# Sharing the first weight load of a DMA-filled decode kernel between two queues

## The chip, the core and the metric

One core of one Trainium2 chip. The metric is the device time of one execution of the kernel in microseconds (us), as a median over runs. All times within the trace are counted from the start of the span, which is about 2 us shorter than the device time of the same run.

## The reference

The reference is one decode step with its gradients: a pre-norm attention block over a sliding window of a key and value cache, then a gated feed-forward block, then the gradient of all eight inputs. Cut to what matters:

```python
D, Hq, Hkv, Sk, Dh, F = 448, 16, 8, 32768, 256, 1792

def _A_ref(x, k_cache, v_cache, wq, wo):
    W = min(4096, max(256, Sk // 4))                 # 4096: only the last W rows are read
    q = (x @ wq).reshape(B, Sq, Hq, Dh) ...
    k = jnp.repeat(k_cache[:, :, Sk - W:, :], rep, axis=1)
    v = jnp.repeat(v_cache[:, :, Sk - W:, :], rep, axis=1)
    p = _softmax(einsum(q, k) * Dh ** -0.5)
    return einsum(p, v).reshape(B, Sq, Hq * Dh) @ wo

h  = x + _A_ref(_layernorm(x), k_cache, v_cache, wq, wo)
h2 = h + _B_ref(_layernorm(h), w_gate, w_up, w_down)   # (x w_gate * x w_up) w_down
# outputs: h2 and the gradients of x, k_cache, v_cache, wq, wo, w_gate, w_up, w_down
```

The gradients of the two caches have the shape of the whole caches, 8 x 32768 x 256 each, and are zero outside the last 4096 rows. Writing those zeros is most of what the kernel moves.

## The kernel before

First, the start: the query weights `wq` come as two pieces (`wqA`, rows of 8 KB, and `wqB`, rows of 4 KB) and the input row `x` behind them, all on SyncE's queue.

```python
    LD = nc.sync
    ZQ = nc.gpsimd
    ...
    nc.vector.memset(ar(0, ZW // 2), 0.0)
    nc.gpsimd.memset(ar(ZW // 2, ZW // 2), 0.0)
    ...
    wq_A = A_wq[0:384, :].rearrange("(c p) j -> p c j", c=3)
    wq_B = A_wq[384:D, :].rearrange("r (h j) -> (r h) j", h=2)
    LD.dma_start(out=wqA, in_=wq_A)
    LD.dma_start(out=wqB, in_=wq_B)
    LD.dma_start(out=x_bf[:], in_=A_x.rearrange("a b d -> (a b) d"))
```

Second, the zero fills. They go out on GpSimd's queue from a zero tile. At the start GpSimd queues 42 tiles of 2 MB from the whole zero tile; then, the last of them at 352 us, it queues 15 more that read only the tile's first half ("half-size fills", whose packets are half as large). The second half of the zero tile is then free for feed-forward weights. When the feed-forward stage is done with it, VectorE clears it and GpSimd queues the rest.

```python
HALF0, HALF1 = 42, 57
...
    send_fills(0, HALF0)               # whole zero tile
    send_fills(HALF0, HALF1, True)     # its first half, twice for each row
    ...
            if n == 1:                 # feed-forward block 1 of 0, 1, 2
                nc.vector.memset(ar(ZW // 2, ZW // 2), 0.0)
                send_fills(HALF1, len(fills) - 1)
```

Third, the feed-forward weights, loaded in three blocks: gate weights and down weights by SyncE, up weights by ScalarE.

```python
    def load_block(n):
        f0, nb, w, wgu, wd = block_views(n)
        for eng, i, wt in ((LD, 0, B_w_gate), (nc.scalar, 1, B_w_up)):
            eng.dma_start(out=wgu[:, 0:3, i, :], in_=wt[0:384, :].rearrange("(c p) f -> p c f", c=3)[:, :, f0:f0 + w])
            eng.dma_start(out=wgu[0:DQ, 3, i, :], in_=wt[384:D, f0:f0 + w])
        LD.dma_start(out=wd, in_=B_w_down[f0:f0 + w, :].rearrange("(p b) n -> p b n", b=nb))

    load_block(0)
    load_block(1)
    ...
            if n + 2 < len(BLOCKS):
                load_block(n + 2)
```

The last gradients are then copied and stored. Five "late" stores of zeros (four of 4 MB, one of 2 MB) are on SyncE's queue; in the trace four of the five are issued behind the last gradients.

Of the kernel before, what the change touches and what calls it, by code (L numbers as in the profile page):

```python
# [34 lines left out]
def kernel(  # L35
        ctx, tc, A_x, A_k_cache, A_v_cache, A_wq, A_wo, B_x, B_w_gate, B_w_up, B_w_down, grad_out,
           out_0, out_1, out_2, out_3, out_4, out_5, out_6, out_7, out_8):
    nc = tc.nc
    LD = nc.sync
# [15 lines left out]
    def ar(off, n):  # L55
        return arena[:, off:off + n]
# [9 lines left out]
    wqA = ar(MB, 24 * KB).rearrange("p (c j) -> p c j", c=3)  # L66
    wqB = ar(MB + 24 * KB, 4 * KB)
# [31 lines left out]
    dh2_bc = const.tile([128, D], bf16)  # L99
    wq_A = A_wq[0:384, :].rearrange("(c p) j -> p c j", c=3)  # L100
    wq_B = A_wq[384:D, :].rearrange("r (h j) -> (r h) j", h=2)
    LD.dma_start(out=wqA, in_=wq_A)
    LD.dma_start(out=wqB, in_=wq_B)
    LD.dma_start(out=x_bf[:], in_=A_x.rearrange("a b d -> (a b) d"))

    ident_bf = const.tile([128, 128], bf16)
# [398 lines left out]
    with tc.tile_pool(name="work2", bufs=2) as work2, tc.tile_pool(name="lnw", bufs=1) as lnw, \  # L505
# [165 lines left out]
        for p0, k, m, w in ((0, 5, 2, 288), (20, 3, 8, ZW), (64, 8, 9, ZW - 40), (0, 4, 8, ZW)):  # L671
            n = k * m * w
            ZQ.dma_start(out=flat[base:base + n].rearrange("(k m f) -> k m f", k=k, m=m),
                         in_=zeros[p0:p0 + 4 * k - 3:4, 0:w].unsqueeze(1).to_broadcast([k, m, w]))
# [35 lines left out]
```

## Time and profile before

| | before |
|---|---|
| median of 3 runs (range) | 793.49 us (793.12 to 794.23) |
| span of the profiled run | 791.1 us |
| bytes moved | 334.75 MB, of which GpSimd's fills 216.01 MB |
| mean rate over the span | 423 GB/s |
| input row arrives | 21.0 us |
| fills resume | 383.3 us |
| last gradient copy starts | 742.8 us |

The prediction below shows the main views. To them belong the share of each engine and the bytes of each queue, from the page of the kernel before (engine, busy us, share of the span, instructions):

```profile
PE 475.9 (60%) x2926; PEld 220.8 (28%) x2926; DVE 410.6 (52%) x621; ACT 196.1 (25%) x309; POOL 29.8 (4%) x41
```

and (queue, packets, MB, share of the 16 DMA engines):

```profile
q1 hardware_dynamic: 11382, 116.68, 35.1%
q10 hardware_dynamic: 1440, 1.61, 0.6%
```

No compute engine is busy for more than about 60% of the span. q1 is SyncE's queue and q10 is ScalarE's.

### The profile page before, as it was taken

How to read it: one execution, taken by the hardware profiler on the slowest of the kernel's cores; microseconds unless marked ns; L12 is line 12 of the kernel's file. 1: busy time of each engine (PE TensorE's matmuls, PEld its weight loads, DVE VectorE, ACT ScalarE, POOL GpSimd, SP SyncE). 2: the span in 40 equal slices, each digit the busy share in tenths (PEclk: the TensorE clock that was granted, in tenths of full speed). 3: DMA queues.
4: the chain of work that ended last, by engine and by line, in shares of the span. 5: the costliest groups of instructions: out<-in, count | busy, mean ns of one | idle time of the engine just before them, and what ended most of it. 6: DMA issues, size and time to landing. Idle time of an engine off the chain costs nothing.

```text
span 791.1 us, 7239 instructions
## 1 busy us (share of the span) xinstructions
PE 475.9 (60%) x2926; PEld 220.8 (28%) x2926; DVE 410.6 (52%) x621; ACT 196.1 (25%) x309; POOL 29.8 (4%) x41
## 2 busy tenths in 40 slices
PE   0359998999999999453226848583551535363100
PEld 0224333344343433142114714231210211131000
DVE  2105764847658476052884288486680583555300
ACT  0043123141241301000101207372331344134300
POOL 6000000000000000110300000000000000001000
PEclk9987999999999999655556959886556556556555
DMA  9999999999999999999999999999999999999998
GB/s 345 429 432 430 429 430 431 432 431 432 428 427 430 427 427 426 418 420 422 433 431 425 425 425 432 427 429 430 427 426 429 428 427 429 423 428 407 413 439 350
DMA packets 28759, 334.75 MB, mean 423 GB/s; under 512 B 1966, under 2 KB 5046, under 8 KB 6966
## 3 DMA queue, kind: packets, MB, share of 16 engines
q0 software_dynamic: 15904, 216.01, 64.2%
q1 hardware_dynamic: 11382, 116.68, 35.1%
q10 hardware_dynamic: 1440, 1.61, 0.6%
q8 instruction: 23, 0.38, 0.2%
q14 instruction: 10, 0.08, 0.0%
HBM read 53.69 MB, written 280.59 MB: 423 GB/s over the span
## 4 chain that ended last, share of the span: by engine, by line
another core or an unknown queue 40%; DMA 25%; DVE 14%; PE 10%; issue 2%; POOL 2%; ACT 1%; DVEq 0%; ACTq 0%; SPq 0%; POOLq 0%
DMA out_dram<-arena 25%; DVE arena L469 2%; PE rows_ps L266 2%; DVE arena L658 2%; DVE arena L554 2%; PE dqb_ps L512 2%; DVE arena L659 2%; PE d_ps L651 2%; PE tr_ps L263 1%; DVE arena L524 1%; DVE arena L438 1%; POOL out_dram L138 1%; PE dqb_ps L515 1%; DVE arena L623 1%
## 5 line engine op out<-in xcount | busy, mean ns | idle before, releaser
L322 DVE TENSOR_TENSOR arena<-arena,p_f 128x2048 bf16<-128x2048 bf16 x64 | 145.4, 2287 | 64.3 <-PE M_ps L327 64.2
L327 PE MATMUL M_ps<-arena 128*128 128x512 bf16 x512 | 129.3, 381 | 0.2 <-ACT arena L333 0.2
L651 PE MATMUL d_ps<-arena 32*128 32x512 bf16 x256 | 45.4, 521 | 100.6 <-DVE arena L659 85.7
L263 PE MATMUL tr_ps<-ident_bf,arena 128*128 128x128 bf16 x1024 | 92.2, 241 | 20.2 <-DMA arena<-in_A_k_cache_dram 12.7
L266 PE MATMUL rows_ps<-arena,vpad 128*16 128x512 bf16 x256 | 89.5, 445 | 21.4 <-DVE arena L623 15.9
L263 PEld LDWEIGHTS <-arena 128*128 128x128 bf16 x1024 | 68.3, 107 | 74.2 <-issue 60.3
L280 ACT COPY arena<-tr_ps 128x1024 bf16<-128x1024 bf16 x64 | 61.8, 1015 | 70.5 <-PE tr_ps L263 70.5
L330 PE MATMUL ok_ps<-arena 128*16 128x512 bf16 x256 | 64.0, 381 | 0.9 <-DVE arena L307 0.9
L655 ACT CAST arena<-d_ps 128x512 bf16<-128x512 f32 x64 | 37.7, 589 | 106.1 <-PE d_ps L651 106.1
L327 PEld LDWEIGHTS <-arena 128*128 128x128 bf16 x512 | 43.3, 99 | 59.2 <-issue 23.4
L621 ACT COPY arena<-tr_ps 128x1024 bf16<-128x1024 bf16 x32 | 32.5, 1016 | 109.9 <-PE tr_ps L263 35.8
L658 DVE CAST arena<-d_ps 128x512 bf16<-128x512 f32 x64 | 43.9, 686 | 18.2 <-PE d_ps L651 17.7
L659 DVE CAST arena<-d_ps 128x512 bf16<-128x512 f32 x64 | 43.6, 681 | 15.5 <-DMA out_dram<-arena 15.5
L651 PEld LDWEIGHTS <-arena 32*128 32x128 bf16 x256 | 10.7, 96 | 126.0 <-issue 81.9
L656 ACT CAST arena<-d_ps 128x512 bf16<-128x512 f32 x64 | 38.1, 595 | 16.8 <-DMA out_dram<-arena 16.8
L266 PEld LDWEIGHTS <-vpad 128*16 128x16 bf16 x256 | 18.7, 91 | 58.4 <-issue 50.6
L330 PEld LDWEIGHTS <-arena 128*16 128x16 bf16 x256 | 19.1, 89 | 41.6 <-issue 20.5
L549 DVE TENSOR_SCALAR arena<-arena,xT 128x1792 bf16<-128x1792 bf16 (+1 forms) x9 | 7.7, 881 | 37.1 <-DMA out_dram<-arena 37.1
L295 ACT ACTIVATE e_f<-cols_ps,nbias 128x32 f32<-128x32 f32 x16 | 4.5, 286 | 86.9 <-DVE nbias L291 86.9
L524 DVE CUSTOM_DVE_ANT_0 arena<-arena 128x4096 bf16<-128x4096 bf16 x3 | 13.1, 4421 | 23.7 <-ACT arena L517 23.7
L268 DVE COPY arena<-rows_ps 16x512 f32<-16x512 f32 x16 | 10.8, 676 | 27.7 <-PE rows_ps L266 27.7
L623 DVE COPY arena<-tr_ps 128x1024 bf16<-128x1024 bf16 x32 | 21.8, 683 | 3.0 <-PE tr_ps L263 2.5
(198 smaller groups left out, 382.2 us busy)
## 6 DMA issues: line engine op xcount, KB each, us to landing
out_dram<-arena POOLq DMA_DIRECT2D x11, 14336.0 KB, 196.1
out_dram<-arena SPq DMA_DIRECT2D x18, 2048.0 KB, 25.6
out_dram<-arena POOLq DMA_DIRECT2D x15, 2048.0 KB, 54.2
arena<-in_A_v_cache_dram SPq DMA_DIRECT2D x10, 2048.0 KB, 52.8
arena<-in_A_k_cache_dram SPq DMA_DIRECT2D x8, 2048.0 KB, 31.3
out_dram<-arena SPq DMA_DIRECT2D x4, 4096.0 KB, 26.1
out_dram<-arena POOLq DMA_DIRECT2D x1, 12288.0 KB, 43.0
out_dram<-arena POOLq DMA_DIRECT2D x1, 8192.0 KB, 337.3
```

The source lines that it names most:

```text
L263: nc.tensor.transpose(tr_ps[:, dh, i, :], X_sb[:, 4 * q + i, dh * 128:(dh + 1) * 128], ident_bf[:])
L266: nc.tensor.matmul(rows_ps[:], lhsT=pad[:, dh, 16 * q:16 * q + 16], rhs=XT[:, dh].rearrange("p t k -> p (t k)"), start=(q == 0 and dh == 0 ...
L280: sT_ps = dots(kv_at(K_off[g]), KT_slot, vpad[g % 2], rows1, ps_c, "cols", lambda q, XT, ps: nc.scalar.copy(out=XT, in_=ps))
L322: nc.vector.tensor_tensor(out=pK, in0=K_sb[:, 4 * c:4 * c + 4, :].unsqueeze(2).to_broadcast([128, 4, 2, Dh]), in1=p_f[:, c::8, :].unsqueez ...
L327: nc.tensor.matmul(M_ps[:, vh, :], lhsT=V_sb[:, t, vh * 128:(vh + 1) * 128], rhs=pK[:, i, :, :].rearrange("p h d -> p (h d)"), start=(t == ...
L330: nc.tensor.matmul(ok_ps[:].rearrange("p k d -> p (k d)"), lhsT=ppad[g % 2][:, 8 * (t % 4) + t // 4, :], rhs=both(g, t), start=(g == 0 and ...
L621: nc.scalar.copy(out=XT, in_=ps)
L651: nc.tensor.matmul(d_ps[:, qi].rearrange("p w d -> p (w d)"), lhsT=rTm[32 * q:32 * (q + 1), l, :], rhs=R_sb[32 * q:32 * (q + 1), :], start ...
L655: nc.scalar.copy(out=stV[:, t:t + 2, :], in_=d_ps[:, :, 0, :])
L656: nc.scalar.copy(out=stK[:, t:t + 2, :], in_=d_ps[:, :, 1, :])
L658: nc.vector.tensor_copy(out=stV[:, t:t + 2, :], in_=d_ps[:, :, 0, :])
L659: nc.vector.tensor_copy(out=stK[:, t:t + 2, :], in_=d_ps[:, :, 1, :])
```

## The change

The intent: the kernel cannot compute before `wq` and `x` are there, and a second queue should bring them sooner. Two of the three chunks of `wqA` stay with SyncE; the third chunk and `wqB` go to ScalarE, which has nothing else to do at that time. No byte is added.

```diff
     wq_A = A_wq[0:384, :].rearrange("(c p) j -> p c j", c=3)
     wq_B = A_wq[384:D, :].rearrange("r (h j) -> (r h) j", h=2)
-    LD.dma_start(out=wqA, in_=wq_A)
-    LD.dma_start(out=wqB, in_=wq_B)
+    LD.dma_start(out=wqA[:, 0:2, :], in_=wq_A[:, 0:2, :])
+    nc.scalar.dma_start(out=wqA[:, 2, :], in_=wq_A[:, 2, :])
+    nc.scalar.dma_start(out=wqB, in_=wq_B)
     LD.dma_start(out=x_bf[:], in_=A_x.rearrange("a b d -> (a b) d"))
```

## The prediction

> **What bounds the kernel now.** I read the page first: its slices, its queue table and its chain. Then I asked for the stretches table, the queue shares in short windows at the start, the timeline of the first 40 us, and the waits.
>
> ```profile
> DMA  9999999999999999999999999999999999999998
> GB/s 345 429 432 430 429 430 431 432 431 432 428 427 430 427 427 426 418 420 422 433 431 425 425 425 432 427 429 430 427 426 429 428 427 429 423 428 407 413 439 350
> ...
> HBM read 53.69 MB, written 280.59 MB: 423 GB/s over the span
> another core or an unknown queue 40%; DMA 25%; DVE 14%; PE 10%; issue 2%; POOL 2%; ACT 1%; DVEq 0%; ACTq 0%; SPq 0%; POOLq 0%
> ```
>
> The 16 DMA engines are busy in every slice and move some 430 GB/s in nearly all of them. 334.75 MB at 430 GB/s would be 778.5 us of the 791.1 us span, so only 12.6 us are lost anywhere. The chain confirms it: 65% of it is transfers, the 40% of unnamed queue included (it lies between GpSimd's issues of zero fills). The fills alone are 216 MB, and they pad every gap that loads and stores leave. Work that comes earlier therefore does not end the kernel earlier. It pays only if it fills one of the places where the DMA engines run low. The stretches table finds them (columns: stretch, its length, busy us of PE, PEld, DVE, ACT, POOL, granted clock, DMA share, GB/s):
>
> ```profile
> 0.00:12.00 12.00, 0.37 (x1) 0.09 (x1) 4.55 (x18) 1.28 (x1) 11.41 (x17) 1.00 0.84 287
> 12.00:20.00 8.00, 0.00 (x0) 0.00 (x0) 0.00 (x0) 0.00 (x0) 0.64 (x1) 1.00 1.02 433
> ...
> 700.00:740.00 40.00, 19.79 (x131) 7.93 (x130) 23.39 (x38) 19.05 (x33) 2.40 (x4) 0.59 1.00 414
> 740.00:745.00 5.00, 0.76 (x8) 0.11 (x4) 2.58 (x4) 2.15 (x4) 0.00 (x0) 0.50 0.84 353
> 745.00:782.00 37.00, 0.00 (x0) 0.00 (x0) 0.00 (x0) 0.00 (x0) 0.00 (x0) 0.50 1.02 438
> 782.00:791.00 9.00, 0.00 (x0) 0.00 (x0) 0.00 (x0) 0.00 (x0) 0.00 (x0) 0.50 0.59 251
> ```
>
> Three losses against 430: the first 12 us lose 12 x (430-287)/430 = 4.0 us; 740 to 745 us lose 5 x (430-353)/430 = 0.9 us; the last 9 us lose 9 x (430-251)/430 = 3.7 us. The change can touch the first directly, the second through the compute chain, and the third hardly (it is the drain of the last stores).
>
> What the weight load looks like today, from the timeline:
>
> ```profile
> 0.75 0.44 SPq L102 DMA_DIRECT2D arena<-in_A_wq_dram  x1
> 0.75 1.28 ACT L179 ACT_TABLE_LOAD   x1 [0.75 <-PEq L694]
> 1.25 0.47 SPq L103 DMA_DIRECT2D arena<-in_A_wq_dram  x1
> 1.77 0.33 SPq L104 DMA_DIRECT2D x_bf<-in_A_x_dram  x1
> ...
> 21.00 0.21 DVE L216 COPY dup<-x_bf 1x128 bf16<-1x128 bf16 x1 [14.27 <-DMA x_bf<-in_A_x_dram]
> ...
> 32.17 1.03 PE L263 MATMUL tr_ps<-ident_bf,arena 128*128 128x128 bf16 x8 [5.02 <-DMA arena<-in_A_k_cache_dram]
> ```
>
> The issue-to-landing view gives 13.1 us for the 3 MB (landed at 13.9) and 19.3 us for the 0.5 MB (20.6). The input row, queued behind both, arrives at 21.0; layernorm and the q matmuls end at 27.2; the first keys land at 32.2. Why half a megabyte needs 6.7 us is in the queue view for 12 to 14 us (queue, packets, MB, share):
>
> ```profile
> q0 software_dynamic: 41, 0.67, 78.3%
> q1 hardware_dynamic: 44, 0.15, 18.6%
> ```
>
> GpSimd's fills (q0) and SyncE's loads (q1) take turns about one packet each, but a fill packet has 16 KB and a packet of these last rows 4 KB. SyncE gets a fifth of the bandwidth exactly while the kernel waits for it. Fill packets show up only from about 10 us on; before, SyncE's queue has the engines to itself.
>
> **What the Trainium skill says.** "DMA: Bandwidth & Descriptors", section "Issuing engines are not separate DMA queues": transfers started by ScalarE, SyncE and GpSimd all run on the same 16 DMA engines and interleave; starting them from several engines saves only issue time. The trace agrees as far as it goes: 430 GB/s whichever mix of queues is active. The same page, "Queues, rings and completion order": each DMA engine goes round-robin between the queues with work, at packet granularity. The 41 to 44 packets above agree with that. "Perfetto Trace Analysis", section "Roofline": a single trn2 core is bounded by its 16 DMA engines at about 435 GB/s; the 428 to 433 of most slices says that there is nothing left to take. "ScalarE: Activation LUTs", section "What ACT_TABLE_LOAD costs": about 1283 ns for the load; the trace has 1.28 us, from 0.75 us, which bears on when ScalarE can issue.
>
> **The change part by part.** No byte is added or removed; there is one DMA issue more (about 0.45 us of a sequencer, by the issues above), and 1.5 of 3.5 MB moves to ScalarE's queue.
>
> Issue: ScalarE has nothing until the layernorm's square root at 21.99 us, so its two issues cost no compute. If they come ahead of the table load they start at 0.75 us, if behind it at 2.03; I take the later as possible. SyncE loses one issue, so everything behind it goes out about 0.5 us earlier, which is nothing as the queue is 20 us deep.
>
> Landing: up to 10 us the loads alone moved 2.83 MB (windows of 1 us, added up). Shared packet by packet, both queues having 8 KB rows at first, ScalarE's third (128 packets, 1.05 MB) and as much of SyncE's are through at 2.1 MB, about 7.5 us. From there 4 KB against 8 KB packets, and about 0.75 MB by 10 us is some 61 of each, so some 67 of each are left. Now fills join: 4 + 8 + 16 = 28 KB a turn, 67 turns are 1.9 MB. At the 0.62 MB that 10 to 12 us moved and 0.43 MB per us after, that takes until about 15 us. So weights and input row should all be there at about 15 us (14 to 17, for the later ScalarE start) instead of 20.6 to 21.0: 5.5 us sooner, an estimate. The gain is from two of three turns instead of one of two. The q chain of 6.2 us then ends at 21 to 22 us; keys, with the same 11.2 us behind the row, land at about 26.5.
>
> Carry-on: from there to 313 us compute is bound by TensorE (99.5 busy us of 100 between 200 and 300), so the 5.5 us lead should mostly survive to the feed-forward stage. There and after it waits mix with DMA landings, and some lead is lost.
>
> Worth at the end: (a) Start-up. The lead takes bandwidth from the fills and gives it back later; that is zero. Only the poor ramp can improve: from 1 to 3 us the single queue moved 0.25 MB where 0.86 would fit, 1.4 us lost. A second queue might keep a second packet in flight and recover part; I take 0.3 us. (b) 740 to 745: fills are exhausted by then, SyncE issues the last gradient stores only when DVE's last copy is done at 742.9, and its last zero stores stand behind them. If compute is some us earlier, this 0.9 us hole closes; I take 0.6. (c) the drain: 0. Sum 0.9 us: 793.5 - 0.9 = 792.6 us.
>
> **The rivals.** First, "the lead counts in full": 5.5 us off, 788 us. For it: TensorE is nearly solid to 313 us and the chain of the last 100 us before 743 passes through compute. Against it: the bytes. After 743 the remaining stores still need 45 us at full rate, and a compute chain that is earlier only leaves fills over for later; to come 5.5 us sooner the mean rate would have to rise, with only the 0.9 us hole and the ramp to rise from. Second, "nothing or slightly worse", 793.5 to 795: the ramp is latency that two queues share, the lead is eaten at waits of the later stages (stores that must land before buffers are free: pieces of 15 to 44 us in the chain), and shifted timing makes a new hole. For it: many such waits. Against it: one delicate place, where fills resume at 383 us after DVE's memset, has half-size fill packets queued until about 390 us, and earlier compute widens that margin. Third, the third queue or the table load delays weights beyond 21 us: the turns argue against it, and a delay of a few us would be hidden in the same way, except that it widens the last hole one for one (795 to 796).
>
> **Range and chances.** The centre is 792.6. Low side: ramp and hole both fully recovered (1.4 + 0.9) and a little more: 790.4. High side: noise of the runs (793.1 to 794.2) and a new hole of about 1 us: 794.8. A change of 2% is 15.9 us, more than all idle DMA time of the kernel, so faster by it is practically excluded (0.01); slower by it would need a stall that no view suggests (0.01); within 2%: 0.98.
>
> **What would show it.** Right: the q copy near 21 to 22 us instead of 27.2 and the first key transposes near 26 to 27; a ScalarE queue at the start with about 1.57 MB; GB/s in the middle unchanged at 428 to 431; 740 to 745 filled or the last copy some us before 742.9; the end nearly the same. Wrong: weights landing at 20 us or later (the turns are not as I read them); a mean rate that moved by more than 1 GB/s; a start-up stretch much above 287 GB/s; new stretches below 400 GB/s in the second half. The prediction as a whole fails if the end moves by more than 3 us either way, which would mean that compute, not bytes, sets it.

## The result

| | before | changed |
|---|---|---|
| median of 6 runs (range) | 793.19 us (792.81 to 794.23) | 793.91 us (793.22 to 795.16) |
| span of the profiled run | 791.1 us | 791.3 us |
| ratio of means | 1 | 1.0009, 95% interval 0.9996 to 1.0022 |

The time is the same.

The page of the changed kernel, rate per slice and queues:

```profile
GB/s 350 428 432 431 430 430 430 432 427 432 427 430 429 427 427 419 423 424 418 415 432 408 430 426 427 432 430 429 427 428 429 427 425 432 420 430 407 429 435 359
...
q1 hardware_dynamic: 11110, 115.10, 34.5%
q10 hardware_dynamic: 1728, 3.18, 1.1%
```

ScalarE's queue gained 1.57 MB, which is the third chunk and `wqB`. The rate is the same nearly everywhere; slices 20 and 22 are lower than before (415 for 433, 408 for 425). The timeline of the changed kernel (start us, us, engine, line, operation, output and inputs, idle time before it and what ended that):

```profile
0.74 0.42 ACTq L103 DMA_DIRECT2D arena<-in_A_wq_dram  x1
...
1.20 0.45 ACTq L104 DMA_DIRECT2D arena<-in_A_wq_dram  x1
...
1.68 1.28 ACT L180 ACT_TABLE_LOAD   x1 [1.68 <-PEq L695]
...
16.94 0.21 DVE L217 COPY dup<-x_bf 1x128 bf16<-1x128 bf16 x1 [12.68 <-DMA x_bf<-in_A_x_dram]
...
24.16 0.19 DVE L238 CAST qT_bf<-qT_ps 128x32 bf16<-128x32 f32 x1 [3.22 <-PE qT_ps L235]
...
27.27 0.71 PE L264 MATMUL tr_ps<-ident_bf,arena 128*128 128x128 bf16 x5 [3.15 <-DMA arena<-in_A_k_cache_dram]
```

ScalarE issues at once and loads its table afterwards. The input row arrives at 16.94 us (before: 21.00), q is finished at 24.35 (27.37), the first keys are transposed from 27.27 (32.17). So the lead is 4.1 us at the row, 3.0 at q and 4.9 at the keys, which are what the next stage waits for.

The queues of the changed kernel from 12 to 14 us (queue, packets, MB, share):

```profile
q0 software_dynamic: 29, 0.48, 55.4%
q1 hardware_dynamic: 31, 0.25, 29.9%
q10 hardware_dynamic: 32, 0.13, 15.9%
```

Three queues take equal turns, and the bytes go as their row sizes, 16 to 8 to 4 KB. The two loading queues now have two turns of three, where SyncE's had one of two.

Where did a lead of 4.9 us go? The stretches table of the changed kernel, in the columns that the prediction explains:

```profile
0.00:12.00 12.00, 0.00 (x0) 0.00 (x0) 3.00 (x11) 1.28 (x1) 11.40 (x17) 1.00 0.85 300
...
388.00:396.00 8.00, 4.42 (x23) 2.52 (x24) 6.32 (x18) 1.23 (x2) 6.44 (x7) 0.50 0.97 400
...
420.00:440.00 20.00, 11.00 (x48) 8.47 (x49) 10.46 (x45) 1.80 (x3) 0.00 (x0) 0.60 1.00 410
...
740.00:745.00 5.00, 0.67 (x8) 0.11 (x4) 2.58 (x4) 2.15 (x4) 0.00 (x0) 0.50 0.97 407
```

and the same stretches of the kernel before that the prediction does not show:

```profile
388.00:396.00 8.00, 2.37 (x15) 1.35 (x13) 5.07 (x7) 1.51 (x4) 1.77 (x3) 0.50 1.03 437
...
420.00:440.00 20.00, 17.28 (x87) 14.25 (x88) 4.18 (x21) 3.40 (x5) 0.00 (x0) 0.76 1.00 424
```

The start is better by 12 x (300-287)/430 = 0.36 us of full rate and 740 to 745 by 5 x (407-353)/430 = 0.63; but 388 to 396 is worse by 8 x (437-400)/430 = 0.69 and 420 to 440 by 20 x (424-410)/430 = 0.65. In this trace a new loss in the middle has taken what the two ends gained; the second trace of the same kernel, told below, shows less of both. (From 420 to 440 us the DMA engines are not idle, the DMA share being 1.00 in both kernels; the packets of 16 KB there take 0.64 us on average where they took 0.62 before, by the packet times in the kept traces, and why is open.) The middle is where the fills resume. SyncE's issues of feed-forward weights show why they resume late. The timeline of SyncE in the kernel before, from 314 to 350 us:

```profile
314.07 1.24 SPq L368 DMA_DIRECT2D arena<-in_B_w_down_dram  x2
315.62 0.38 SPq L366 DMA_DIRECT2D arena<-in_B_w_gate_dram  x1
321.82 0.47 SPq L367 DMA_DIRECT2D arena<-in_B_w_gate_dram  x1
349.84 0.34 SPq L368 DMA_DIRECT2D arena<-in_B_w_down_dram  x1
```

and in the changed kernel, from 310 to 350 us:

```profile
310.75 35.92 SPq L369 DMA_DIRECT2D arena<-in_B_w_down_dram  x3
346.97 0.96 SPq L367 DMA_DIRECT2D arena<-in_B_w_gate_dram  x1
347.99 1.85 SPq L368 DMA_DIRECT2D arena<-in_B_w_gate_dram  x1
```

Before, SyncE issues two down loads, then block 1's gate weights at 316 and 322 us, and block 2's down load when its buffer is free at 350. In the changed kernel, block 2's down load stands directly behind the other two. It has to wait some 35 us for its buffer, and block 1's gate weights wait behind it until 347. Nothing in the diff says so. Comparing the order of each engine's instructions in the two traces shows that the scheduler, which places the instructions in each engine's stream when the kernel is built, placed several things differently after the edit: this down load on SyncE; on ScalarE, block 0's four broadcast copies ahead of block 1's up loads (the first up issue is at 347.57 instead of 340.19); at the start on VectorE, six small reductions and a copy behind the first steps of the layernorm (this makes the stretch from the input row to the copy of q 7.2 us long, where it was 6.2 before). So the attention stage ended 3.3 us sooner (VectorE's copy of its result at 310.55 instead of 313.87), and the feed-forward stage threw that away. GpSimd's first issue after the pause, from the timeline of the kernel before:

```profile
383.29 5.71 POOL L142 DMA_DIRECT2D out_dram<-arena  x6 [30.72 <-DVE arena L443]
```

and of the changed kernel:

```profile
389.56 6.47 POOL L143 DMA_DIRECT2D out_dram<-arena  x7 [39.27 <-DVE arena L444]
```

A lead of 3.3 us at 310 became a lag of 6.3 us at the point where the fills resume. After that the lag melts again: first stores of cache gradients at 500.97 against 494.57, then at 678.92 against 675.54, the last ones at 742.84 against 742.93.

### The profile page after: what moved, and what is told of

Same layout as the page of the kernel before. It is cut to its first block, busy times and chain, and to the rows that moved or that the text cites. A ratio compares the mean times of both kernels' runs of the same rounds, so it can differ in the third digit from the quotient of the medians. Undisturbed runs are those within 1.5% of the kernel's fastest.

```text
span 791.3 us, 7240 instructions
## 1 busy us (share of the span) xinstructions
PE 467.9 (59%) x2926; PEld 219.6 (28%) x2926; DVE 410.2 (52%) x621; ACT 195.9 (25%) x309; POOL 29.7 (4%) x41
## 4 chain that ended last, share of the span: by engine, by line
another core or an unknown queue 40%; DMA 27%; DVE 13%; PE 8%; issue 2%; POOL 2%; ACT 1%; SPq 0%; DVEq 0%; ACTq 0%; POOLq 0%
DMA out_dram<-arena 27%; DVE arena L470 2%; PE dqb_ps L513 2%; DVE arena L555 2%; DVE arena L659 2%; PE d_ps L652 1%; PE rows_ps L267 1%; DVE arena L660 1%; DVE arena L525 1%; POOL out_dram L139 1%; PE tr_ps L264 1%; DVE arena L439 1%; PE dqb_ps L516 1%; POOL out_dram L143 1%
## 5 line engine op out<-in xcount | busy, mean ns | idle before, releaser
L264 PE MATMUL tr_ps<-ident_bf,arena 128*128 128x128 bf16 x1024 | 90.6, 238 | 19.7 <-DMA arena<-in_A_k_cache_dram 12.1
L267 PE MATMUL rows_ps<-arena,vpad 128*16 128x512 bf16 x256 | 86.2, 431 | 22.2 <-DVE arena L624 16.1
L269 DVE COPY arena<-rows_ps 16x512 f32<-16x512 f32 x16 | 10.8, 675 | 27.6 <-PE rows_ps L267 27.6
L421 PE MATMUL gu_ps<-X_b,arena 128*128 128x1 bf16 x112 | 9.6, 186 | 24.6 <-DMA arena<-in_B_w_gate_dram 23.6
```

Of the source, the lines that this page charges most:

```text
L264: nc.tensor.transpose(tr_ps[:, dh, i, :], X_sb[:, 4 * q + i, dh * 128:(dh + 1) * 128], ident_bf[:])
L267: nc.tensor.matmul(rows_ps[:], lhsT=pad[:, dh, 16 * q:16 * q + 16], rhs=XT[:, dh].rearrange("p t k -> p (t k)"), start=(q == 0 and dh == 0 ...
```

## The experiments

Three questions were open. What did the new order cost, and was it what hid a gain? Is a compute lead worth anything at the end if it does survive? And does the lead need a second queue? The theory ("bytes"): the end is set by the bytes that 16 DMA engines have to move, and earlier compute pays only where it fills a stretch in which they run low. The rival ("compute"): the lead would count if the reordering did not eat it.

Where an experiment had to hold an instruction behind another in the scheduler's order without adding a wait, it used this helper:

```python
    def behind(later, earlier):
        tc.add_manual_dep(later.ins, earlier.ins.name,
            mybir.DependencyInfo(mybir.DependencyClass.NoSync, mybir.DependencyReason.DATA), reason="order")
```

All runs gave correct outputs, all had five timed rounds, and in each of the two sets the kernels shared one chip and the runs of the kernel before (medians 793.45 and 793.44 us, 9 runs each, 792.85 to 794.15 over both).

| run | median us (range) | ratio to before | 95% interval |
|---|---|---|---|
| c1_after_again | 793.20 (792.95 to 794.63) | 1.0003 | 0.9991 to 1.0016 |
| e1_sync_order | 792.97 (792.81 to 793.64) | 0.9997 | 0.9984 to 1.0009 |
| e3_order_alone | 796.67 (795.44 to 797.19) | 1.0039 | 1.0026 to 1.0051 |
| e4_more_half_fills | 794.25 (793.82 to 794.54) | 1.0009 | 0.9995 to 1.0023 |
| e5_both_orders | 792.87 (792.41 to 794.30) | 0.9997 | 0.9984 to 1.0009 |
| e7_rows_swapped | 793.36 (792.65 to 793.96) | 1.0001 | 0.9987 to 1.0015 |
| e6_late_zeros | 793.01 (792.88 to 793.80) | 0.9997 | 0.9985 to 1.0010 |
| e8_fewer_half_fills | 797.81 (796.45 to 798.10) | 1.0053 | 1.0040 to 1.0065 |

### The changed kernel again

No edit.

> The changed kernel once more, as the yardstick of this chip. Both theories: 793.5 to 794.3 us, ratio to the kernel before 1.000 to 1.002. The spread of this run says how small a difference the other three can settle.

Measured: 793.20 us, ratio 1.0003. Together with the first result the changed kernel has 11 runs: seven from 792.95 to 793.93 and four from 794.58 to 795.16. Both profiled runs fell in the lower part (resumption at 389.56 and 388.31), so what the upper four are is open. The median lies just below the expected 793.5 to 794.3. The result stands: the same time, perhaps a trace slower.

The second trace is also the measure of what one trace can say. The same kernel now shows 295 GB/s up to 12 us (300 in the first trace), 419 from 388 to 396 (400), 421 from 420 to 440 (410) and 373 from 740 to 745 (407). Differences of a few tenths of a microsecond between two traces are therefore no findings by themselves. One trend holds over the runs with 15 half-size fills: the later the fills resume, the thinner the stretch from 388 to 396 us. It moved 437 GB/s for a resumption at 383.29, 434 at 384.71, 419 at 388.31, 400 at 389.56 and 271 at 392.94.

### SyncE's order put back

The changed kernel, with block 2's down load held behind block 1's gate weights.

```diff
-            eng.dma_start(out=wgu[0:DQ, 3, i, :], in_=wt[384:D, f0:f0 + w])
-        LD.dma_start(out=wd, ...)
+            marks[n, i] = eng.dma_start(out=wgu[0:DQ, 3, i, :], in_=wt[384:D, f0:f0 + w])
+        down = LD.dma_start(out=wd, ...)
+        if n == 2:
+            behind(down, marks[1, 0])
```

> The changed kernel with one ordering edge: SyncE's load of block 2's down weights again goes out behind block 1's gate weights, as in the kernel before; nothing else moves. Order theory (the split itself gains about a third of a us at the start; the changed order of SyncE's queue turned a lead of 3.3 us into a lag of 6.3 us at the fills' resumption and let the fill queue run thin at 388 to 392 us): fills resume at 378 to 381 us instead of 389.6, 388 to 392 us is back at 428 to 434 GB/s, time 792.0 to 792.9, ratio to before 0.9985 to 1.000, so 1.0 to 1.8 us below the changed kernel. Rival one (three interleaved queues or noise, the order is harmless): 793.5 to 794.3, same as the changed kernel. Rival two (the early lead counts in full once nothing eats it): below 790.5.

Measured: 792.97 us, ratio 0.9997. Gate weights now go out at 312.32 and 318.19 us, and the fills resume at 384.71, not at 378 to 381 as expected. ScalarE still issued block 1's up weights at 347.5, behind block 0's copies, and SyncE's second gate load of block 2 then stood 10.0 us behind up weights that were still in flight, as SyncE's waits say (line waited at, what it waited for, total us, times, longest):

```profile
SPq L372 <- DMA arena<-in_B_w_up_dram: 10.0, 1, 10.0
```

So putting SyncE's order back brings the resumption forward by 4.9 us, and putting ScalarE's back as well, in the run of both orders below, by 3.7 us more. The two are not shares of a sum: in the next run SyncE's order alone, put into the kernel before, delays the resumption by 9.7 us. From 388 to 396 us the rate is back at 434 GB/s. The median lies just above the 792.0 to 792.9 of the order theory, with the ratio inside its range, and differs from the changed kernel's by less than the intervals: the run shows the mechanism, not a gain.

### The order alone

The kernel before, with its one-queue load, but with block 2's down load traced ahead of block 1's gate weights and these held behind it. One tail of block 1's up loads moved on ScalarE too, from 340.61 to 351.54 us, so "alone" holds but for that. The edit, condensed:

```diff
-    load_block(0)
-    load_block(1)
+    load_gu(0); load_down(0); load_down(1)
...
-            if n + 2 < len(BLOCKS):
-                load_block(n + 2)
+            if n == 0:
+                down2 = load_down(2)
+                load_gu(1, down2)      # both gate loads behind(down2)
+                load_gu(2)
```

> The kernel before, with its one-queue load, but with SyncE's queue in the changed order (block 2's down weights ahead of block 1's gate weights). Order theory: no lead to start from, so fills resume 9 to 10 us later than in the kernel before, at 392 to 394 us, when the old fills (which end at about 391 us) are gone: a dry stretch of 2 to 4 us, time 794.5 to 797.5, ratio 1.0015 to 1.005. Rival one (order harmless): ratio 0.999 to 1.001.

Measured: 796.67 us, 3.2 above before, ratio 1.0039, inside the expected range. GpSimd's resumption in the timeline of this run:

```profile
392.94 5.69 POOL L146 DMA_DIRECT2D out_dram<-arena  x6 [41.93 <-DVE arena L456]
```

and the stretch around it in its stretches table:

```profile
388.00:396.00 8.00, 2.02 (x5) 0.56 (x6) 7.48 (x20) 0.12 (x1) 3.06 (x4) 0.50 0.65 271
```

The queued half-size fills are used up, and the stretch loses 8 x (437-271)/430 = 3.1 us of full rate. It is not the whole account of the profiled run, whose span is 3.6 us above before: some 1.1 us more is lost up to 440 us (421 GB/s for 431 to 420 us, then 412 for 424), and 740 to 745 us, now at 419 GB/s, gives 0.8 us back. Still the reading is clear: SyncE's part of the order that the scheduler chose costs about three microseconds when there is no early lead to pay for it, and most of the cost is bytes not moved while the fill queue is dry. In the changed kernel the lead of 3.3 us moved the same order from 392.9 to 389.6, about where the queued fills end.

### More half-size fills

The changed kernel with its order kept and four more half-size fills queued, so that the queue cannot run dry.

```diff
-HALF0, HALF1 = 42, 57
+HALF0, HALF1 = 42, 61
```

> The changed kernel with its changed order kept, but 19 instead of 15 fills sent as half-size ones ahead of the feed-forward stage: 8 MB, about 19 us, more fill work queued before the point where fills resume. Order theory with the fill queue as the carrier of the cost: resumption still at about 389.6 us, but no thin stretch at 388 to 392 us; time 0.5 to 1.5 us below the changed kernel, ratio to before 0.9985 to 1.0003. If the order costs in another way than through the fill queue (a later compute chain as such): no gain, ratio 1.000 to 1.002 as the changed kernel.

Measured: 794.25 us, ratio 1.0009: a miss, and inside the range of the other reading (no gain). The thin stretch did go (427 GB/s from 388 to 396, 421 from 420 to 440, for 400 and 410 in the first trace of the changed kernel, 419 and 421 in the second), but the end did not move by the 0.5 to 1.5 us expected. The time came back elsewhere: 740 to 745 us fell to 302 GB/s, from 407 (373 in the second trace), which is 5 x (407-302)/430 = 1.2 us. This reads as bytes that were moved from the end to the middle: with the last copy no earlier (it starts at 743.82 us here), there is less left over to fill the hole before it. So this run does not show that the dry queue cost the changed kernel anything; that a dry queue can cost is shown by the run before and by the last one.

### Both orders put back

The second run of orders: SyncE as above, and on ScalarE block 0's copies held behind block 1's up loads. From the feed-forward stage on, every engine has the order of the kernel before; only the start is new.

```diff
-                    nc.scalar.copy(out=dgb[...], in_=bc_ps[:, 0:w // 2])
+                    ev = nc.scalar.copy(out=dgb[...], in_=bc_ps[:, 0:w // 2])
+                    if n == 0:
+                        behind(ev, marks[1, 1])
```

> The changed kernel with two ordering edges: SyncE's order as in the run before last, and on ScalarE block 1's up-weight loads again ahead of block 0's four copies, as in the kernel before. From the feed-forward stage on every engine now has the order of the kernel before. Order theory: the lead of 3.3 us at 310 us is kept to the resumption of the fills, 379 to 381 us. For the end two readings. Bytes: the lead is worth at most the hole at 740 to 745 us and the start, 792.3 to 793.1 us, ratio 0.9988 to 0.9998. Compute (the last stores go out when the last copy is done, and 47 us of stores follow, so a lead that survives counts in full): 790 to 791, ratio 0.996 to 0.9975. If the lead has melted by 742 us the bytes reading is right.

Measured: 792.87 us, ratio 0.9997. The lead now survives: fills resume at 381.06 (2.2 us ahead of before), the first gradient stores go at 490.97 (3.6 ahead), and the last copy starts at 738.48 (4.3 ahead):

```profile
381.06 4.73 POOL L147 DMA_DIRECT2D out_dram<-arena  x5 [28.01 <-DVE arena L453]
```

The hole of the prediction is closed, as the stretches table of this run shows:

```profile
740.00:745.00 5.00, 0.00 (x0) 0.00 (x0) 0.00 (x0) 0.00 (x0) 0.00 (x0) 0.50 1.01 424
745.00:782.00 37.00, 0.00 (x0) 0.00 (x0) 0.00 (x0) 0.00 (x0) 0.00 (x0) 0.50 1.01 432
782.00:791.00 9.00, 0.00 (x0) 0.00 (x0) 0.00 (x0) 0.00 (x0) 0.00 (x0) 0.50 0.55 233
```

And the end is where it was: a span of 791.2 us. This run decides between the theories. Compute finishes 4.3 us earlier and the kernel does not; the compute reading, which wanted 790 to 791 us and a ratio of at most 0.9975, falls outside the interval (from 0.9984 up). It also shows that the hole was worth less than it looked. 0.82 us more of full rate between 740 and 745 (5 x (424-353)/430) are followed by 432 instead of 438 GB/s to 782 us (37 x 6/430 = 0.52 us less) and 233 instead of 251 in the drain (0.38 less).

### One queue, rows swapped

The kernel before, with the piece of short rows first. No second queue. Apart from the two loads themselves, no instruction changed its place.

```diff
-    LD.dma_start(out=wqA, in_=wq_A)
     LD.dma_start(out=wqB, in_=wq_B)
+    LD.dma_start(out=wqA, in_=wq_A)
```

> The kernel before, one queue, with its two weight loads in the other order: the 4 KB rows first, when no fills compete, the 8 KB rows after. All engines' orders but these two loads stay. Packet-turn theory: by 10 us 2.83 MB are through, so some 100 packets of 8 KB are left and take turns with 16 KB fill packets: about 6 us, weights and input row there at 16 to 17 us, as with two queues (16.9), first keys at 27 to 28 us. So the second queue is not needed for the lead. If two queues are needed: input row at 19 us or later. Time: 792.3 to 793.3, ratio 0.9985 to 1.0005 in any case (bytes).

Measured: 793.36 us, ratio 1.0001. The input row arrives at 16.04 us, sooner than with two queues, and q is done at 22.4. From the timeline of this run:

```profile
16.04 0.21 DVE L216 COPY dup<-x_bf 1x128 bf16<-1x128 bf16 x1 [9.31 <-DMA x_bf<-in_A_x_dram]
```

and its queues from 12 to 14 us:

```profile
q0 software_dynamic: 36, 0.59, 68.7%
q1 hardware_dynamic: 35, 0.28, 32.9%
```

Turns are still one each, but SyncE's rows have 8 KB in this stretch, so it moves 0.28 MB where it moved 0.15. The short rows had gone through before the fills came. The reading by packet turns, from which 16 to 17 us had been expected, holds; the first keys came at 28.26, a little after the 27 to 28 expected, and the median lies just above its range. The lead is again there at the resumption (380.56) and at the last copy (739.26), and again the end does not move. The start moves 299 GB/s up to 12 us, as the two-queue runs do (295 to 307), so that small gain is not the second queue's either.

### A late store moved forward

The swapped kernel with 4 MB of the late zeros sent just ahead of the last two gradient stores, so that the engines have work whatever the copies do. The helper holds the store in its place; those lines are left out.

```diff
                 nc.vector.memset(ar(ZW, ZW), 0.0)
+                early = LD.dma_start(out=zero_rows(out_3, G - 1, 0, 2, 2 * ZW)[0], in_=ar(0, 2 * ZW))
...
-    late_jobs = [..., (out_3, G - 1, 0, 6, 2 * ZW), ...]
+    late_jobs = [..., (out_3, G - 1, 2, 6, 2 * ZW), ...]
```

> The swapped loads, and one of the last 4 MB zero stores is moved ahead of the last two gradient stores on SyncE, so that the DMA engines have work while DVE finishes its last copies. Bytes theory: the hole at 740 to 745 us closes (420 GB/s and up), the last copy stays at 742 to 743 us, time 0.5 to 1.3 us below the kernel before: 792.0 to 792.9, ratio 0.9983 to 0.9995. If compute sets the end: the time after the last copy gets 10 us shorter or the copy moves, and the total changes by more than 2 us.

Measured: 793.01 us, ratio 0.9997. The stretch from 740 to 745 moved 437 GB/s, which is all that the engines take elsewhere, and the last copy started at 739.08 (742 to 743 had been expected, but the swap already brings it to 739). No gain is clear of the noise, and the median lies just above the expected range. To close what remained of the hole after the swap (421 GB/s) added nothing that the runs can resolve.

### Fewer half-size fills

The kernel before with two half-size fills fewer, and nothing late in compute: a dry queue without a lag.

```diff
-HALF0, HALF1 = 42, 57
+HALF0, HALF1 = 42, 55
```

> The kernel before, all orders kept, but 13 instead of 15 half-size fills ahead of the feed-forward stage: 4 MB, 9.8 us, less fill work queued. They end at about 381 us while GpSimd resumes at about 383 us. If a dry fill queue is what costs: a stretch below 300 GB/s between 381 and 388 us, and time up by 1 to 4 us (the hole at 740 to 745 us takes 0.9 us back): 794.5 to 797, ratio 1.0013 to 1.005. If the lag of compute costs, not the dry queue: ratio 0.999 to 1.001.

Measured: 797.81 us, 4.4 above before, ratio 1.0053; a little over the expected range. The fills resume where they did before, 382.57, and the last copy starts at 742.77. The expected thin stretch is there (274 GB/s from 380 to 388 us). The stretches table of the kernel before, then of this run:

```profile
370.00:388.00 18.00, 6.27 (x53) 4.39 (x54) 11.58 (x27) 1.01 (x1) 4.71 (x5) 0.50 1.01 428
...
370.00:388.00 18.00, 6.70 (x56) 4.91 (x57) 11.73 (x27) 1.01 (x1) 5.42 (x7) 0.50 0.87 356
```

So 18 x (428-356)/430 = 3.0 us are lost here, and 20 x (424-409)/430 = 0.7 from 420 to 440; 740 to 745 us, at 429 GB/s, gives 5 x (429-353)/430 = 0.9 back. The profiled run was the fastest of the five, 796.45 us, and its span is 3.6 us above before. Compute is on time and the kernel is 4.4 us later. With the run of both orders this is the pair that settles the bound: earlier compute gives nothing that the runs resolve, and a dry fill queue in the middle costs time with compute on schedule.

## Why the prediction was right or wrong, point by point

- **The bound (right).** The DMA engines set the end. A lead at the last copy of 4.3 us (both orders put back) or 3.5 us (one queue, rows swapped) was worth less than the runs can resolve; a dry fill queue in the middle went with 3.2 and 4.4 us more.
- **Packet turns (right; size a little off).** The row was put at 15 us (14 to 17) and came at 16.9. The turns themselves were predicted well: the last packets of the two loads end at 15.0 and 15.2 us in the recorded packet times. But the loads are reported as landed only at 16.2 and 16.3, and the more than 1 us between last packet and landing was missing. Keys were put at 26.5 and came at 27.3. The assumption that ScalarE might issue only after its table load was not needed: it issued at 0.74.
- **The q copy (off, without effect).** Put at 21 to 22 us, it came at 24.2, because VectorE's small reductions had been placed inside the layernorm chain. It did not count, as the keys came later still.
- **"The 5.5 us lead should mostly survive to the feed-forward stage" (right up to there).** 3.3 us arrived at 310 us.
- **"Earlier compute widens that margin" at the resumption of the fills (wrong).** This is the step that failed. The prediction took the order of instructions as given. The scheduler had moved loads of the feed-forward stage, the margin shrank by 6.3 us (5.0 in the second trace), and thinner stretches appeared (400 and 410 GB/s; 419 and 421 in the second trace). Of its two rivals the second, "nothing or slightly worse", with "shifted timing makes a new hole", describes what was seen, though by another cause than the ones it named.
- **Term (a), 0.3 us for the start (right in size).** 300 GB/s for 287 is 0.36 us, 295 in the second trace 0.22, 296 and 297 in the repaired versions 0.25 and 0.28. But the one-queue swap has it too, so "a second packet in flight" is not the shown cause.
- **Term (b), 0.6 us for the hole from 740 to 745 (wrong as a term).** In the changed kernel the hole filled by 0.63 us (0.23 in the second trace), but not through an earlier last copy (742.84 for 742.93 at the store issue). It reads as filled by bytes that the middle had left over: summed over the stretches, the changed kernel was some 0.7 MB behind at 440 us and still some 0.4 to 0.5 MB at 740. Where the copy did come earlier the hole closed as foreseen, and most of it was given back by 791 us. The three runs with the hole closed (both orders, rows swapped, late zeros) have ratios of 0.9997, 1.0001 and 0.9997, 0.1 to 0.2 us on average. The prediction took a stretch in which the DMA engines run low as time that can be won at the end. What was won here was lost again in the last microseconds (see below), and the term should have been near 0.
- **The sum.** 792.6 us predicted, 793.91 measured, 793.20 in the repeat: inside the range of 790.4 to 794.8 and within 2%. The bound carries this, not the terms: a forecast of no change at all would have come no less near, and whether the small difference is a gain or a loss is not resolved (0.9996 to 1.0022).

Why does a closed hole not shorten the end? The views show the mean of the DMA engines, but the kept traces have the recorded start and duration of every packet, and so how many packets are under way at a time: 16 through nearly all of the span. In the hole of the kernel before the count really falls, to some 8 for a short while, so the hole is not late counting. Missing packets, taken as time of all 16, come to 0.67 us in the hole and 1.48 us at the very end. With the hole closed they are 0 there, but 2.58 us at the end (both orders), 2.04 (rows swapped) and 2.59 (late zeros). The count now first falls for good at 783.8 us (both orders) where it fell at 787.7 before, while the last packet ends at 789.8 for 789.5. So the time won in the hole comes back as a more uneven finish: some DMA engines are done earlier, and not the last one. This is what the traces show; a packet's record does not name its engine, and why the finish is less even stays open.

Also open are the four slower runs of the changed kernel, and the slower packets from 420 to 440 us.

No version beat the kernel before beyond noise. If a lead at the start were wanted for its own sake, the swap of two lines gives it without a second queue and without disturbing the order.

## What to carry to other kernels

Before counting on a lead, ask where in the kernel the bounding resource runs low, and whether the lead can fill that place; if it is busy everywhere, earlier work elsewhere ends nothing earlier. And a dip in the rate is not yet time to win: here a hole of 0.9 us was closed three times, and nothing that the runs resolve came of it. After any edit, compare the instruction order of the built program with the old one, engine by engine: here two moved loads at the start changed the order of loads 300 us later, and SyncE's part of that order costs 3.2 us in a kernel that has no lead. And where queues share DMA engines by turns, put short rows where nothing competes and keep a margin of queued fill ahead of any point at which filling pauses.

## What the Trainium skill lacked or had wrong

- "DMA: Bandwidth & Descriptors", section "Queues, rings and completion order", has the round-robin by packets, of some 9 to 17 descriptors each. It does not say what this makes of the bandwidth of queues with different rows. Here what the profile counts as a packet was one row: 29, 31 and 32 packets in 2 us moved 0.48, 0.25 and 0.13 MB, so the queue with rows of 4 KB had a quarter of the bytes of the one with 16 KB. Loading the short rows first brought the input row from 21.0 to 16.0 us.
- The same page, section "Latency and other measured facts", gives about 1 us to the first byte for transfers that GpSimd issues. Here GpSimd's first fill was issued from 5.13 us on, in a group of six issues of about 1 us each, and the first fill packets are counted only after 10 us, in both kernels. The packet records put the start of the first one at 10.8 us (10.4 in the changed kernel), and a packet of 16 KB takes about 0.6 us, so the way of counting does not explain 5 us; no run here isolates the cause.
- No page has it: a small edit can change the order in which a scheduler places instructions on other engines, far from the edit. Here SyncE, ScalarE, VectorE and TensorE all changed, and GpSimd's fills resumed at 389.6 instead of 383.3 us.
